# A long-convolution and feed-forward kernel on one core: later start of TensorE in the list, a tile of its own for one sum, and a longer time taken for transposing transfers

## The chip, the core and the metric

The kernel runs on one NeuronCore of a Trainium2 chip. The metric is the time of one execution in device microseconds (us). A core has five engines that run their own instruction queues side by side and wait for one another by semaphores: TensorE (PE; weight loads are shown apart as PEld), VectorE (DVE), ScalarE (ACT), GpSimd (POOL) and SyncE (SP), which here issues most transfers; POOL issues those that add to their destination.

## The reference

```python
x = A_q                                    # 2048 x 1024
xn = _layernorm(x, axis=-1)
return x + _A_ref(xn, A_k, A_v, A_shift_k, A_ssm_k, A_ssm_D) + _B_ref(xn, B_w1, B_w2)
# _A_ref: k_shift = causal depthwise convolution of k with 4 taps; kv = k_shift * v
#         y = causal convolution of kv with ssm_k over the whole length (by FFT) + kv * ssm_D
#         result xn * y
# _B_ref: silu(xn @ w1) @ w2, w1 of 1024 x 3584, w2 of 3584 x 1024
```

## The kernel before

The work is one long program for PE. The two products of the feed-forward part are made in float16 with a high and a low half of each factor: every matmul of 128 x 512 stands three times (lines L1030, L1031, L1032 for the first product, L1183, L1184, L1185 for the second). The first product is made by seven products of sums of blocks, the second is mostly plain. The long convolution goes by group of 128 channels (eight groups): a forward transform on PE (L1670, L1671, L1672), a product of spectra on DVE, a transform back on PE (L1863, L1864, L1865), and a gate. Its work stands between that of the feed-forward part and keeps DVE busy while PE multiplies.

At the start, 16 tiles of 128 rows of x (`xt`) and the pieces of w1 are loaded. DVE takes the statistics of a tile (L565, L568), normalises it (L602), PE transposes it in two times four 128 x 128 steps (L621), ACT and DVE split the result into the high and low float16 halves `x` (L353 is DVE's). The scale of a piece of w1 comes from its sum of squares: ACT makes most of these sums, DVE makes that of the second piece (`squares_dve`, L796, L799, L800) and writes it into one column of the tile `ss`; PE adds them over the partitions (L464, L467), and DVE takes a power of two from it (L508, L510).

The order of all instructions is made when the program is built, by the class `Order`. Each piece of work is a generator, a stream with a bias, and yields operations with an engine, an estimated busy time (`busy`), an estimated time until the result is there (`late`), and the tiles that it reads and writes. In each step the stream with the smallest possible start time less its bias gives its operation, which is emitted at once; the estimates of free engines, written and read cells of 256 bytes, and of one common transfer pipe (`pipe`) are moved on. So the estimates set the order on every engine, and nothing else: on the chip each instruction waits by semaphores for what it needs.

Three places of this matter here.
- Until the first product begins, the list fills gaps that it sees on PE with constant matmuls of 128 x 512 (L1937), `int((t - free - 0.1) / 0.22)` of them before an operation. PE begins with 18 float32 matmuls (`warm_up`, L1934; each is two passes), estimated at 0.3 us.
- Later, before the first matmul of a product, a gap in the estimate is filled in part with matmuls of zeros (L333).
- `X` (L343) is a transfer on SP's queue that transposes: in each group it turns the scaled signal `cm` into the tile `hl`, which PE's forward transform reads. `L` (L338) is a plain transfer on the same queue, which runs in order: wo (halves of the weights), wraw (raw weights), hsfA, hsfS (stores of the first product's result), xg (rows of x for the gate). `G` (L347) is a transfer on POOL's queue that adds a tile to the output, after the gate multiplication `yt` (L353), and after the last step of a part of the second product, `hf`.

A part of the first product ends with ACT copying its banks of PSUM (`hf<-ff`, L361), DVE subtracting or adding another bank to it (`hf<-ff,hf`, L350), ACT's Silu, and a split into halves (`ht`, ACT L361 and DVE L353). The forward transform's banks `ps` are read by ACT (`spec<-ps`) and DVE (`tmp<-tmp,ps`, `spec<-spec,ps`).

Of the kernel before, what the change touches and what calls it, by code (L numbers as in the profile page):

```python
# [11 lines left out]
F32 = mybir.dt.float32  # L12
BF16 = mybir.dt.bfloat16
# [7 lines left out]
P = 128  # L21
# [69 lines left out]
class Op:  # L91


    def __init__(self, eng, busy, late, emit, reads, writes, margin, nbytes=0):
        self.eng, self.busy, self.late, self.emit, self.margin = eng, busy, late, emit, margin
        self.reads, self.writes, self.nbytes = reads, writes, nbytes
        self.table = self.fill = None


class Stream:  # L100
# [5 lines left out]
class Order:  # L106
# [60 lines left out]
    def run(self):  # L167
        while self.streams:
            for s in list(self.streams):
                if not isinstance(s.head, Op) and s.head():  # L170
                    self.advance(s)
            best = None
            for s in self.streams:
                if isinstance(s.head, Op):
                    t = max(self.free[s.head.eng], s.at)
                    if best is None or t - s.bias < best[0]:
                        best = t - s.bias, t, s
            assert best is not None, "the streams wait for one another"
            _, t, s = best
            op, (r, w) = s.head, s.touched  # L180
            if self.spare is not None and op.eng == "PE":
                op.fills = max(0, int((t - self.free["PE"] - 0.1) / 0.22))
                for _ in range(op.fills):
                    self.spare()
            elif op.fill is not None and t > 45.0:
                for _ in range(int(((t - self.free[op.eng]) * 0.7 - 0.3) / 0.22)):
                    op.fill()
            op.emit()
            if op.table not in (None, self.table):
                op.busy += 1.28  # L190
                self.table = op.table
            done = t + op.busy
            end = done + op.late
            if op.nbytes:
                self.pipe = max(self.pipe, t + (2.0 if t < 3.0 else 3.0)) + op.nbytes / (265e3 if t < 3.3 else 330e3)
                done = end = max(end, self.pipe + 0.2)
            self.free[op.eng] = t + op.busy
            for c in r:
                self.read[c] = max(self.read.get(c, 0.0), done)
            for c in w:  # L200
                self.wrote[c] = end, op.eng
            self.now = max(self.now, end)
            self.advance(s)
# [94 lines left out]
def h3_ffn_kernel(ctx, tc, x, kp, vs, fs, shift, dskip, w1, w2, cfwd, cinv, out):  # L298
    nc = tc.nc
    ctx.enter_context(tc.manual_schedule())  # L300
    order = Order()
# [26 lines left out]
    def T(f, o, ins, us, m=0.1, start=None, **kw):  # L328

        p = Op("PE", us, 0.3, f, ins, [o], m)  # L330
        if start is not None:
            z = o[:, 0:1] if len(o.shape) == 3 else o[:, 0:P]
            p.fill = lambda: nc.tensor.matmul(z, zeros, ones, start=start, stop=start, **kw)  # L333
        return p

    def L(o, i, m=0.3):
        n = size(o) * o.shape[0] * mybir.dt.size(o.dtype)
        return Op("SP", 0.4, 0.1, lambda: nc.sync.dma_start(o, i), [i], [o], m, n)  # L338

    def X(o, i, m=0.3):  # L340

        n = size(o) * o.shape[0] * mybir.dt.size(o.dtype)
        return Op("SP", 0.6, 4.0, lambda: nc.sync.dma_start(o, i, transpose=True), [i], [o], m, n)  # L343

    def G(o, i, m=0.3):
        n = size(i) * i.shape[0] * mybir.dt.size(i.dtype)
# [107 lines left out]
    def total(ring, ss, n, margin, joined=False):  # L454

        yield ring.ready
        pt, tok = ring.tile([P, W])
        yield pw.ready
        e, etok = pw.tile([P, 4])
        high = ss.bitcast(BF16)[:, 1::2]  # L460

        def mm():
            if joined:
                nc.tensor.matmul(pt[:, 0:1], onesb, tinyb, start=True, stop=False)  # L464
                for q in range(n):
                    w = manyb if n == 4 and q in (1,) else onesb
                    nc.tensor.matmul(pt[:, 0:1], w, high[:, q:q + 1], start=False, stop=q == n - 1)  # L467
            else:
                nc.tensor.matmul(pt[:, 0:n], onesb, high, start=True, stop=True)
        yield T(mm, pt[:, 0:n], [ss], 0.12 + 0.04 * n * joined, m=margin)  # L470
        return pt, tok, e, etok

    def norm(ring, ss, ns, then, flags, margin=1.5):
# [296 lines left out]
    def load_pair(n):  # L770
# [10 lines left out]
        for a in range(len(pieces)):  # L781
# [7 lines left out]
            yield L(raws[n][2][a], w1r[:, ks, cols])  # L789
            flag["raw", n, a].set()  # L790

    def squares_dve(r, o):
        st = lnp.tile([P, 1, 6], F32, name="wst", bufs=1)
        mean = lnp.tile([P, 2], F32, name="wmean", bufs=1)
        flat = r.rearrange("p k w -> p (k w)")
        yield V(lambda: nc.vector.bn_stats(st[:, 0, :], flat), st, [r], us=0.65)  # L796

        def chain():
            nc.vector.bn_aggr(mean, st)  # L799
            nc.vector.scalar_tensor_tensor(o, mean[:, 0:1], mean[:, 0:1], mean[:, 1:2], op0=MUL, op1=ADD)  # L800
        yield V(chain, o, [st], us=0.45)

    def scales_w1():
        for n, (_, i) in enumerate(pairs):
            yield (0.25, 0.2, 0.1, 0.05)[min(n, 3)]
            m = 4 if n == 0 else 2
            if n >= NP:
                for a in range(m):
                    yield flag["raw", n, a]
                flag["scaled", n].set()  # L810
                continue
            yield sq_r.ready
# [1117 lines left out]
    def warm_up():  # L1930

        pt, tok = ff.tile([P, 4, P])
        for _ in range(18):
            yield T(lambda: nc.tensor.matmul(pt[:, 0, :], ones, ones, start=True, stop=True), pt[:, 0, :], [], 0.3)  # L1934

        def constants():
            nc.tensor.matmul(pt.rearrange("p a b -> p (a b)"), onesb, oneb.to_broadcast([P, W]), start=True, stop=True)  # L1937
        order.spare = constants
        yield flag["first"]
        order.spare = None  # L1940
        tok.set()
# [64 lines left out]
```

## Time and profile before

| | us |
|---|---|
| median of 3 runs | 1242.58 |
| lowest, highest | 1242.13, 1243.62 |
| profiled execution | 1246.58 |
| its span, first to last instruction | 1244.8 |
| PE busy in it | 1230.2 |
| DVE busy in it | 1122.5 |
| ACT busy in it | 741.8 |

The mean granted clock of TensorE is 0.999 of full speed over the span. Times in the views are counted from the span's start. A row of a timeline gives the start, the length, engine, line, operation, output and inputs by the program's names, and in brackets the idle time of the engine before it and what ended that. A row of the waits gives who waited for whom, the total, the count and the longest. A row of the windows gives the stretch, its length, the busy times (and counts) of PE, PEld, DVE, ACT and POOL, the granted clock, the busy share of the transfer engines, and GB/s. A busy matmul is shown with its whole latency, so successive ones overlap: what a matmul costs is the distance from start to start.

### The profile page before, as it was taken

Reading aid. Unit: us, or ns where it says so; the run is one execution under the profiler, and the core shown is the slowest. Engines: PE = TensorE matmul, PEld = TensorE weight load, DVE = VectorE, ACT = ScalarE, POOL = GpSimd, SP = SyncE. Lnnn points to the kernel's source line nnn. Section 1 sums busy time; section 2 is a strip of 40 time slices with the busy share of each in tenths; the row PEclk is TensorE's granted clock in tenths of the full one; section 3 lists DMA queues with packets and bytes.
Section 4 is the critical chain, followed back from the end, with each engine's and each line's share of the span. In section 5 each row is a group of like instructions: output and inputs, shape, how many; then the busy total and the mean of one; then the engine's idle time right before and its main releaser. Section 6 shows DMA issues by size and latency. Waiting matters only on the chain.

```text
span 1244.8 us, 17311 instructions
## 1 busy us (share of the span) xinstructions
PE 1230.2 (99%) x6144; PEld 598.5 (48%) x6144; DVE 1122.5 (90%) x1367; ACT 741.8 (60%) x1299; POOL 142.2 (11%) x164
## 2 busy tenths in 40 slices
PE   9999999999999999999999999999999999999998
PEld 7645544444444544445444544544454454445444
DVE  7999997888799869998999799799989979998993
ACT  6878887877767767768663632653263265426231
POOL 1100000000000120002010300300030030113114
PEclk9999999999999999999999999999999999999999
DMA  9289889889999898969997887788596688978777
GB/s 338 69 267 320 300 299 314 280 276 352 304 350 285 254 246 263 286 208 259 352 315 207 185 244 169 166 263 243 127 220 164 133 177 240 251 144 138 162 150 102
DMA packets 254438, 293.21 MB, mean 236 GB/s; under 512 B 48784, under 2 KB 167824, under 8 KB 252176
## 3 DMA queue, kind: packets, MB, share of 16 engines
q1 hardware_dynamic: 227760, 267.46, 68.6%
q0 software_dynamic: 26592, 24.65, 15.3%
q8 instruction: 48, 0.79, 0.3%
q14 instruction: 38, 0.31, 0.1%
HBM read 193.48 MB, written 98.57 MB: 235 GB/s over the span
## 4 chain that ended last, share of the span: by engine, by line
PE 68%; DVE 19%; DMA 6%; issue 4%; ACT 2%; POOL 0%; SPq 0%; DVEq 0%; ACTq 0%; POOLq 0%
PE ff L1031 10%; PE ff L1030 10%; PE ff L1032 10%; PE ff L1183 10%; PE ff L1184 10%; PE ff L1185 9%; DVE spec L350 7%; DVE tmp L350 3%; DMA hf<-in_w 2%; DVE x L353 2%; PE ps L1670 1%; PE ps L1672 1%; PE ps L1671 1%; DVE spec L353 1%; DMA out<-yt 1%
## 5 line engine op out<-in xcount | busy, mean ns | idle before, releaser
L1183 PE MATMUL ff<-x,wo 128*128 128x512 f16 (+2 forms) x872 | 329.0, 378 | 2.1 <-ACT hf L361 2.1
L1184 PE MATMUL ff<-x,wo 128*128 128x512 f16 (+2 forms) x872 | 329.2, 378 | 0.0
L1185 PE MATMUL ff<-x,wo 128*128 128x512 f16 (+2 forms) x872 | 329.0, 378 | 0.0
L1030 PE MATMUL ff<-x,wo 128*128 128x512 f16 (+2 forms) x840 | 306.7, 367 | 1.8 <-ACT hf L361 1.8
L1031 PE MATMUL ff<-x,wo 128*128 128x512 f16 (+2 forms) x840 | 306.8, 367 | 1.1 <-DVE x L353 1.1
L1032 PE MATMUL ff<-x,wo 128*128 128x512 f16 (+2 forms) x840 | 306.8, 367 | 0.0
L350 DVE TENSOR_TENSOR spec<-spec 128x1024 f32<-128x1024 f32 (+2 forms) x272 | 263.0, 999 | 2.3
L1184 PEld LDWEIGHTS <-wo 128*128 128x128 f16 x872 | 85.4, 98 | 102.1 <-issue 3.2
L1185 PEld LDWEIGHTS <-wo 128*128 128x128 f16 x872 | 85.5, 98 | 101.9 <-issue 0.7
L1183 PEld LDWEIGHTS <-wo 128*128 128x128 f16 x872 | 85.5, 98 | 101.2 <-issue 0.8
L1032 PEld LDWEIGHTS <-wo 128*128 128x128 f16 x840 | 82.2, 98 | 92.0 <-issue 1.2
L1030 PEld LDWEIGHTS <-wo 128*128 128x128 f16 x840 | 82.2, 98 | 88.1 <-issue 0.2
L1031 PEld LDWEIGHTS <-wo 128*128 128x128 f16 x840 | 82.2, 98 | 88.1 <-issue 2.1
L347 POOL DMA_DIRECT2D out<-hf x59 | 52.3, 888 | 449.2 <-ACT hf L361 339.4
L347 POOL DMA_DIRECT2D out<-yt x56 | 63.7, 1359 | 336.9 <-DVE yt L353 192.8
L361 ACT ACTIVATE hf<-ff,invc 128x512 f32<-128x512 f32 x60 | 40.9, 682 | 99.6 <-PE ff L1185 79.0
L350 DVE TENSOR_TENSOR tmp<-spec 128x2048 f32<-128x2048 f32 (+1 forms) x48 | 92.5, 1932 | 0.9
L353 DVE SCALAR_TENSOR_TENSOR ht<-hf,wsc,ht 128x1024 f16<-128x1024 f32 (+1 forms) x56 | 67.3, 1202 | 11.7 <-ACT ht L361 11.5
L361 ACT ACTIVATE spec<-spec 128x1024 bf16<-128x1024 f32 x32 | 33.7, 1054 | 68.5 <-DVE spec L350 68.4
L353 DVE SCALAR_TENSOR_TENSOR wo<-raw,wsc,wo 128x512 f16<-128x512 f32 (+1 forms) x56 | 56.3, 1011 | 12.3 <-ACT wo L361 12.0
L361 ACT ACTIVATE spec<-ps 128x512 f32<-128x512 f32 x96 | 55.0, 589 | 16.3 <-PE ps L1672 15.0
L361 ACT ACTIVATE ht<-hf,wsc 128x1024 f16<-128x1024 f32 (+1 forms) x56 | 60.7, 1085 | 4.7 <-DVE hf L350 3.0
(187 smaller groups left out, 1756.1 us busy)
## 6 DMA issues: line engine op xcount, KB each, us to landing
wo<-hs SPq DMA_DIRECT2D x160, 256.0 KB, 4.0
hs<-ht SPq DMA_DIRECT2D x80, 256.0 KB, 4.4
wraw<-in_w SPq DMA_DIRECT2D x31, 512.0 KB, 5.3
out<-hf POOLq DMA_DIRECT2D x59, 256.0 KB, 4.4
raw<-in_w SPq DMA_DIRECT2D x28, 512.0 KB, 5.9
kin<-in_kp SPq DMA_DIRECT2D x16, 704.0 KB, 5.9
kf<-in_fs SPq DMA_DIRECT2D x8, 1024.0 KB, 5.8
hl<-in_vs SPq DMA_DIRECT2D x32, 256.0 KB, 6.2
```

The costliest lines, as they stand in the source:

```text
L347: return Op("POOL", 1.1, 4.8, lambda: nc.gpsimd.dma_start(o, i, accum_op=ADD), [i], [o], m, n)
L350: return V(lambda: nc.vector.tensor_tensor(o, a, b, op=op), o, [a, b], **k)
L353: return V(lambda: nc.vector.scalar_tensor_tensor(o, a, s, b, op0=op0, op1=op1), o, [a, b] + ([] if isinstance(s, float) else [s]), **k)
L361: nc.scalar.activation(o, i, func, scale=scale, **kw)
L1030: nc.tensor.matmul(o, w[:, 0, k], xf[:, :, k, 0], start=first and k == 0, stop=False, **kw)
L1031: nc.tensor.matmul(o, w[:, 0, k], xf[:, :, k, 1], start=False, stop=False, **kw)
L1032: nc.tensor.matmul(o, w[:, 1, k], xf[:, :, k, 0], start=False, stop=last and k == KH - 1, **kw)
L1183: nc.tensor.matmul(o, hx[:, n, 0, :], wc[:, n, 0, q], start=first and n == 0, stop=False, **kw)
L1184: nc.tensor.matmul(o, hx[:, n, 0, :], wc[:, n, 1, q], start=False, stop=False, **kw)
L1185: nc.tensor.matmul(o, hx[:, n, 1, :], wc[:, n, 0, q], start=False, stop=last and n == 3, **kw)
L1670: nc.tensor.matmul(o, cf[:, 0], hi[i], start=i == 0, stop=False, **kw)
L1671: nc.tensor.matmul(o, cf[:, 0], lo[i], start=False, stop=False, **kw)
```

## The change

Three things are changed. The list takes PE to be free only from 1.0 us on, and a matmul of the warm-up to take 0.36 us and not 0.3. DVE's sum of squares gets a tile of its own, `wsum`, in place of a column of `ss`, so that the list's cell of 256 bytes no longer holds ACT's sums and DVE's at once; PE reads it there. And an operation has a field `extra`, which is added to the end that the transfer pipe gives: 1.0 us for each transposing transfer, 0 for all others.

```diff
@@ class Op
         self.table = self.fill = None
+        self.extra = 0.0
@@ Order.run
             if op.nbytes:
                 self.pipe = max(self.pipe, t + (2.0 if t < 3.0 else 3.0)) + op.nbytes / (265e3 if t < 3.3 else 330e3)
-                done = end = max(end, self.pipe + 0.2)
+                done = end = max(end, self.pipe + 0.2 + op.extra)
@@ h3_ffn_kernel
+    def later(p, extra):
+        p.extra = extra
+        return p
+
     def X(o, i, m=0.3):
-        return Op("SP", 0.6, 4.0, lambda: nc.sync.dma_start(o, i, transpose=True), [i], [o], m, n)
+        return later(Op("SP", 0.6, 4.0, lambda: nc.sync.dma_start(o, i, transpose=True), [i], [o], m, n), 1.0)
@@ total
-                    w = manyb if n == 4 and q in (1,) else onesb
-                    nc.tensor.matmul(pt[:, 0:1], w, high[:, q:q + 1], start=False, stop=q == n - 1)
+                    w, v = (manyb, wsum.bitcast(BF16)[:, 1:2]) if n == 4 and q == 1 else (onesb, high[:, q:q + 1])
+                    nc.tensor.matmul(pt[:, 0:1], w, v, start=False, stop=q == n - 1)
@@ scales_w1
+    wsum = lnp.tile([P, 1], F32, name="wsum")
...
-                    yield from squares_dve(r, ss[:, a:a + 1])
+                    yield from squares_dve(r, wsum)
@@ warm_up
-            yield T(lambda: nc.tensor.matmul(pt[:, 0, :], ones, ones, start=True, stop=True), pt[:, 0, :], [], 0.3)
+            yield T(lambda: nc.tensor.matmul(pt[:, 0, :], ones, ones, start=True, stop=True), pt[:, 0, :], [], 0.36)
@@ the streams
     add(begin(), 0.05)
+    order.free["PE"] = 1.0
     add(warm_up(), 0.0)
```

Counted over the program, 24 constant matmuls (L1937) stand where 31 stood, and three zero fills (L333) where two stood; all other counts are the same. Lines of the changed kernel stand 5 to 8 further down.

The first place is PE's queue at the start, around the transposes of the first row tile (`xt`, two times four steps into `ft`). Before:

```order
L1937 MATMUL ff_217<-oneb 128x512
L621 MATMUL ft_295<-ident,xt_216 128x128 x4
L621 MATMUL ft_322<-ident,xt_216 128x128 x4
L1937 LDWEIGHTS oneb
...
L464 LDWEIGHTS oneb
L464 MATMUL ft_334<-tinyb,oneb 128x1
L467 LDWEIGHTS oneb
L467 MATMUL ft_334<-ss_220,oneb 128x1
L467 LDWEIGHTS many
L467 MATMUL ft_334<-ss_220,many 128x1
```

Now:

```order
L1944 MATMUL ff_218<-oneb 128x512
L626 MATMUL ft_295<-ident,xt_217 128x128 x4
L626 MATMUL ft_318<-ident,xt_217 128x128 x4
L1944 LDWEIGHTS oneb
...
L469 LDWEIGHTS oneb
L469 MATMUL ft_308<-tinyb,oneb 128x1
L472 LDWEIGHTS oneb
L472 MATMUL ft_308<-ss_221,oneb 128x1
L472 LDWEIGHTS many
L472 MATMUL ft_308<-wsum,many 128x1
```

The pieces are the same; what moved is the number of constant matmuls around them, all of which read as the first row does: 13 ahead of the transposes, 6 between them and the sums, 12 behind before, and 4, 2 and 18 now.

The second place is DVE's queue in the middle of the program, from the second gate multiplication of a group on (`yt`; `hf` subtracts a bank of the first product, `ht` is a low half of its result, `spec` and `tmp` are parts of the spectra). Before:

```order
L353 SCALAR_TENSOR_TENSOR yt_3191<-ps_4151,csc_2138,xg_3366 128x512
L350 TENSOR_TENSOR tmp<-tmp,ps_4130 128x2x256
L353 SCALAR_TENSOR_TENSOR zl_4187<-spec,csc_2138,zh_4186 128x1024
L350 TENSOR_TENSOR tmp<-tmp,ps_4137 128x2x256
L350 TENSOR_TENSOR spec<-spec 128x2x512 x2
L353 SCALAR_TENSOR_TENSOR yt_3191<-ps_4185,csc_2138,xg_4162 128x512
L350 TENSOR_TENSOR spec<-spec,ps_4197 128x2x256
L350 TENSOR_TENSOR spec<-spec,ps_4227 128x2x256
L353 SCALAR_TENSOR_TENSOR ht_201<-hf_200,wsc,ht_201 128x8x128
L353 SCALAR_TENSOR_TENSOR yt_3191<-ps_4216,csc_2138,xg_4250 128x512
L350 TENSOR_TENSOR hf_198<-ff_4030,hf_199 128x512
```

Now:

```order
L358 SCALAR_TENSOR_TENSOR yt_3157<-ps_4158,csc_2132,xg_3280 128x512
L358 SCALAR_TENSOR_TENSOR zl_4190<-spec,csc_2132,zh_4189 128x1024
L355 TENSOR_TENSOR tmp<-tmp,ps_4138 128x2x256
L355 TENSOR_TENSOR tmp<-tmp,ps_4145 128x2x256
L355 TENSOR_TENSOR spec<-spec 128x2x512 x2
L358 SCALAR_TENSOR_TENSOR ht_201<-hf_200,wsc,ht_201 128x8x128
L355 TENSOR_TENSOR spec<-spec,ps_4205 128x2x256
L355 TENSOR_TENSOR spec<-spec,ps_4220 128x2x256
L355 TENSOR_TENSOR hf_198<-ff_4015,hf_199 128x512
L358 SCALAR_TENSOR_TENSOR yt_3157<-ps_4188,csc_2132,xg_4169 128x512
```

The third yt now stands behind ht, two sums and hf, all of which stood behind it before; the fourth comes five rows further down.

The third place is SP's queue around a group's last transposing transfer, at the passage from the first product to the second (`wraw` are raw weights, `wo` halves of weights, `hsfA` and `hsfS` stores of results). Before:

```order
L338 DMA hsfA_69<-ht_201 128x4x256
L338 DMA xg_5242<-in_x 128x2x128 x2
L343 DMA_TRANSPOSE hl_2134<-cm 128x8x128
L338 DMA wraw_3192<-in_w 128x2x512
L338 DMA hsfA_72<-ht_202 128x4x256
L338 DMA wo_194<-hs_73 128x1024 x2
L338 DMA hsfS_67<-ht_201 128x4x256
```

Now:

```order
L339 DMA hsfA_69<-ht_201 128x4x256
L339 DMA wraw_3158<-in_w 128x2x512
L339 DMA hsfA_72<-ht_202 128x4x256
L339 DMA wo_194<-hs_73 128x1024 x2
L339 DMA xg_5246<-in_x 128x2x128 x2
L348 DMA_TRANSPOSE hl_2129<-cm 128x8x128
L339 DMA hsfS_67<-ht_201 128x4x256
```

The transfer and the load of xg ahead of it moved behind a load of raw weights, a store and two loads of weights.

More of the change, by code (lines that the diff above doesn't have):

```diff
@@ L465, in mm @@
                 for q in range(n):
-                    w = manyb if n == 4 and q in (1,) else onesb
-                    nc.tensor.matmul(pt[:, 0:1], w, high[:, q:q + 1], start=False, stop=q == n - 1)
+                    w, v = (manyb, wsum.bitcast(BF16)[:, 1:2]) if n == 4 and q == 1 else (onesb, high[:, q:q + 1])
+                    nc.tensor.matmul(pt[:, 0:1], w, v, start=False, stop=q == n - 1)
             else:
                 nc.tensor.matmul(pt[:, 0:n], onesb, high, start=True, stop=True)
-        yield T(mm, pt[:, 0:n], [ss], 0.12 + 0.04 * n * joined, m=margin)
+        yield T(mm, pt[:, 0:n], [ss, wsum] if n == 4 else [ss], 0.12 + 0.04 * n * joined, m=margin)
         return pt, tok, e, etok
```

## The prediction

> **What bounds the kernel now.** I read the page first: its busy times and its chain.
>
> ```profile
> PE 1230.2 (99%) x6144; PEld 598.5 (48%) x6144; DVE 1122.5 (90%) x1367; ACT 741.8 (60%) x1299; POOL 142.2 (11%) x164
> ...
> PE 68%; DVE 19%; DMA 6%; issue 4%; ACT 2%; POOL 0%; SPq 0%; DVEq 0%; ACTq 0%; POOLq 0%
> ```
>
> TensorE (PE) is busy for 99% of the span. Its matmuls do not get faster by this change, so only two things can move the time: matmuls that fall away, and waits of PE that go or come. Hence the second view, the waits of PE over the whole span.
>
> ```profile
> PE ps L1670 <- ACT tmp L361: 2.7, 2, 1.7
> PE ff L1183 <- ACT hf L361: 2.1, 1, 2.1
> PE ff L1030 <- ACT hf L361: 1.8, 1, 1.8
> PE ff L1031 <- DVE x L353: 1.1, 1, 1.1
> PE ff L1934 <- DVE oneb L404: 1.1, 1, 1.1
> PE ps L1670 <- DVE tmp L350: 0.7, 1, 0.7
> PE ps L1670 <- DVE yt L353: 0.3, 1, 0.3
> ```
>
> Seven rows, 9.8 us in all. That is the whole stake of the re-ordering; anything better needs fewer matmuls. The third view is PE's timeline at the start, where the change takes matmuls away.
>
> ```profile
> 1.06 6.61 PE L1934 MATMUL ff<-one 128*128 128x128 f32 x36 [1.06 <-DVE oneb L404]
> 7.51 3.00 PE L1937 MATMUL ff<-oneb 128*128 128x512 bf16 x13
> 10.35 1.04 PE L621 MATMUL ft<-ident,xt 128*128 128x128 f32 x8
> 11.22 1.47 PE L1937 MATMUL ff<-oneb 128*128 128x512 bf16 x6
> 12.53 0.17 PE L464 MATMUL ft<-tinyb,oneb 128*128 128x1 bf16 x1
> ...
> 12.66 2.78 PE L1937 MATMUL ff<-oneb 128*128 128x512 bf16 x12
> 15.28 1.03 PE L621 MATMUL ft<-ident,xt 128*128 128x128 f32 x8
> 16.15 0.22 PE L1030 MATMUL ff<-x,wo 128*128 128x128 f16 x1
> ...
> 19.32 0.22 PE L1031 MATMUL ff<-x,wo 128*128 128x128 f16 x1 [1.10 <-DVE x L353]
> ```
>
> The columns are start, length, line, operation, count. From 7.51 to 16.15 PE never idles, but 31 of its matmuls (13, 6 and 12 of L1937) compute nothing: they are put in while the list believes that PE has nothing to do.
>
> **Term 1: the start.** The order of the changed kernel has 4, 2 and 18 constants in the three places. One costs (10.35 - 7.51) / 13 = 0.218 us from start to start. DVE's timeline tells whether the data are there earlier:
>
> ```profile
> 7.31 0.80 DVE L602 TENSOR_SCALAR xt<-xt,ln 128x1024 f32<-128x1024 f32 x1
> ...
> 9.00 1.40 DVE L565 BATCH_NORM_STATS2 st<-xt 128x6 f32<-128x512 f32 x2 [0.55 <-DMA xt<-in_x]
> ...
> 13.46 0.69 DVE L353 SCALAR_TENSOR_TENSOR x<-ft,x 128x512 f16<-128x512 f32 x1 [0.23 <-ACT xt L361]
> 14.07 0.81 DVE L602 TENSOR_SCALAR xt<-xt,ln 128x1024 f32<-128x1024 f32 x1
> ```
>
> The first tile is normalised at 7.31 + 0.80 = 8.11, and the eight transposes wait behind constants until 10.35. With four constants they start at 7.51 + 4 x 0.218 = 8.38, take 11.22 - 10.35 = 0.87, and end at 9.25; two constants and the norm (0.44 + 0.13) bring PE to 9.82, where the norm before was at 12.53. Eighteen constants then fill to 9.82 + 3.92 = 13.74. Is the second tile ready by then? DVE now does half of the statistics (0.7) from 9.00, the first low half of x (0.69), the other statistics, the small norm steps, the second low half (0.69) and the normalisation (0.81): some 4.2 us of work in a row, 13.2 at best, against 14.88 before. So the constants, not DVE, release the transposes, at 13.74 instead of 15.28: **-1.53 us** (7 x 0.218). The first product L1030 moves from 16.15 by as much, and the wait of 1.10 at 19.32 hangs on DVE work behind the same transposes and moves along. A little more is possible, since DVE is ahead by 1.7 and PE by 1.5: I bound this term by -2.0. On the other side it could be 0, if an input lands too late (a rival below).
>
> The own tile for DVE's sum of squares (`wsum`) only frees the list from a dependence that it saw inside one 256-byte cell; the instructions are the same length, so it costs 0 by itself. The three zero matmul fills (L333) in place of two:
>
> ```profile
> L333 PE MATMUL ff<-one,zero x4: 273/273/275, 316.7 to 317.0; 128*128 128x128 f32 x4
> ```
>
> Four passes lie between 316.7 and 317.0, about 0.11 us each, two to a fill. One fill more is **+0.22 us**; all three now stand near 568 and not at 316, so 0.45 is gained early and 0.67 spent late.
>
> **Term 2: the waits at 441 and 455.** Only between 283 and 990 us does the larger completion time re-order anything. DVE, ACT, PE and the chain of waits between 430 and 457:
>
> ```profile
> 442.25 8.19 DMA out<-yt
> ```
>
> ```profile
> 431.35 0.75 DVE L353 SCALAR_TENSOR_TENSOR yt<-ps,csc,xg 128x512 f32<-128x512 f32 x1
> ...
> 440.54 0.75 DVE L353 SCALAR_TENSOR_TENSOR yt<-ps,csc,xg 128x512 f32<-128x512 f32 x1 [2.65 <-DMA out<-yt]
> ...
> 450.62 0.75 DVE L353 SCALAR_TENSOR_TENSOR yt<-ps,csc,xg 128x512 f32<-128x512 f32 x1 [3.39 <-DMA out<-yt]
> 451.28 0.68 DVE L350 TENSOR_TENSOR hf<-ff,hf 128x512 f32<-128x512 f32 x1
> ```
>
> ```profile
> 452.00 1.15 ACT L361 ACTIVATE hf<-hf,wsc 128x1024 f32<-128x1024 f32 x1 [3.20 <-DVE hf L350]
> ...
> 456.31 0.57 ACT L361 ACTIVATE hf<-ff 128x512 f32<-128x512 f32 x1
> ```
>
> ```profile
> 454.72 0.38 PE L1032 MATMUL ff<-x,wo 128*128 128x512 f16 x1
> 456.94 0.38 PE L1030 MATMUL ff<-x,wo 128*128 128x512 f16 x1 [1.84 <-ACT hf L361]
> ```
>
> The third and fourth gate multiplications (yt) wait for the store of the one before, which is out of the way only 440.54 - 431.35 = 9.2 us after it began (8.19 of a transfer in the chain's row). DVE runs in order: behind the fourth stands the subtraction hf, behind it ACT, behind that the bank which PE wants. So a store costs PE 456.94 - 454.72 - 0.22 = 2.00 us, and the third yt, on whose bank PE waits at 441, 0.45. In the changed order hf stands **ahead** of both, and the work that followed the third yt (the subtractions of two products, one ht) stands ahead of it too. Counting PE's rows there at 0.216 us a matmul, with the 1.53 and 0.45 that PE is ahead, the product that hf reads is complete near 442, so hf runs near 443 and ACT's step some 9 us before 452.00. The third yt comes after about 6.7 us more of DVE work, and the store has landed. The fourth may still wait (the store behind it lands near 452), but behind it stand only spectrum sums, no bank of PE. **-2.45 us**.
>
> What is late next? After 456 DVE hardly rests:
>
> ```profile
> 460.00:520.00 60.00, 60.00 (x281) 27.20 (x280) 59.76 (x69) 41.19 (x73) 0.00 (x0) 1.00 0.83 256
> 520.00:580.00 60.00, 59.32 (x295) 28.61 (x294) 58.41 (x76) 41.36 (x65) 2.20 (x2) 1.00 0.80 236
> ```
>
> The third busy column is DVE's: 59.76 of 60, then 58.41. There PE's lead lasts only if DVE has it too. Of its idle time before 456 DVE loses 1.5 with the start and, by its rows, the 2.65 at 440; it reaches the same work about 4 us earlier, as PE does. So I leave the later waits (0.7 and 1.0 at 578 and 688, 1.7 at 900, 2.1 at 1085) as they are: PE's order after 690 is nearly the same, and these hang on DVE and ACT alone.
>
> **Sum.** -1.53 - 2.45 + 0.22 = -3.76 us. The profiled execution took 1246.58 (span 1244.8, 1.8 around it), which becomes 1242.8. It lies 4.0 above the median of the runs, 1242.58; part of that is this:
>
> ```profile
> 1088.00:1092.00 4.00, 4.00 (x12) 1.49 (x11) 3.96 (x5) 0.00 (x0) 0.88 (x1) 0.57 0.55 70
> ```
>
> ```profile
> 1088.14 0.63 PE L1184 MATMUL ff<-x,wo 128*128 128x512 f16 x1
> ...
> 1091.13 0.52 PE L1185 MATMUL ff<-x,wo 128*128 128x512 f16 x1
> ```
>
> After the 2.12 us of waiting at 1085 the granted clock falls to 0.57 for some 3 us: seven starts take 2.99, 0.427 each and not 0.216, about 1.7 us lost in all. After the 1.84 at 455 there was no such loss. I carry the difference over to the median unchanged: 1242.58 - 3.76 = **1238.8 us**.
>
> [...]
>
> **Rivals.**
>
> *DVE keeps what PE wins* (0.18). If DVE meets 456 only 1.5 us earlier, the two waits at 578 and 688 grow by the 2.45 and only the start remains: 1242.58 - 1.53 + 0.22 = 1241.3. For it speak the windows above; against it that DVE's idle time at 440 is before the subtraction and shrinks in the new order.
>
> *The start does not do what it says* (0.12). An input still in flight could hold the first product, PE then idling where constants were. The row at 9.00 shows DVE waiting 0.55 for such a transfer. Then 1242.58 - 2.45 + 0.22 = 1240.35, and with term 2 lost as well (half of this case) 1242.8.
>
> *More goes* (0.10). The list now gives each transposing transfer a later end, so work that needs one stands later; the waits at 578 and 688 (0.7 and 1.0) could go too: 1238.8 - 1.7 = 1237.1.
>
> *The sync queue blocks the weights* (0.20), the case on the other side. SP's queue is in order, and near 562 to 575 the changed order puts a weight load, a store of ht parts and two loads of wo ahead of the transposing transfer and its xg.
>
> ```profile
> SPq L338 <- DVE ht L353: 5.6, 3, 2.2
> ```
>
> ```profile
> wo<-hs SPq DMA_DIRECT2D x160, 256.0 KB, 4.0
> ```
>
> A store waits up to 2.2 us for its ht; what stands behind it then needs 4.0 us to land (a wo) or more (the transfer). Here, at the passage from the first product to the second, where all loads are ordered anew, PE would wait 2.2 + 4.0 = 6.2 us once the lead of the weights is used up, and with the slow clock after it 1.7 more: 1238.8 + 6.2 = 1245.0 to 1246.7. It decides from the point at which a wo lands after its matmul's turn. Against it: no wait of PE on a transfer stands among the seven rows; and the moved transfer, issued near 572.5 - 4 in the changed order, is used some 10 us later.
>
> **How the numbers follow.** The forecast has 0.40, the rivals 0.18, 0.12, 0.10 and 0.20. A measurement of this kernel can tell about 0.2%, 2.5 us, from no change. Faster by more than that: the forecast, "more goes", and a quarter of the start rival, 0.53. Within it: "DVE keeps", the rest of the start rival, 0.27. Slower: 0.20. The range goes down to "more goes" with the start at its bound of -2.0 (1236.6) and up to the lower price of the blocked queue (1245.1), leaving out less than 2 in 10.
>
> **What would show it.** Term 1: eight transposes near 8.4 and again near 13.7, and the first L1030 near 14.6. Term 2: no row of PE waiting for ACT hf with L1030, none for DVE yt, and hf ahead of a waiting yt. "DVE keeps": the rows of PE on tmp grow to 4 us. The queue: a row of PE or of its weight loads on DMA wo. I am wrong if a wait of PE over 2 us stands where none was, or if the first L1030 still starts near 16.

## The result and the profile after

The changed kernel takes 1239.08 us (median of 9 runs, 1237.92 to 1240.01), beside 1242.58 (1239.97 to 1245.04, 9 runs) of the kernel before on the same chip. The ratio is 0.9968 with the 95% interval [0.9958, 0.9978]: 4.0 us faster (2.7 to 5.2; the two medians differ by 3.5), where 3.76 were forecast. The sum came out; several of its terms did not. The profiled execution took 1238.71, its span is 1236.9.

The page of the changed kernel, busy times and chain:

```profile
PE 1226.6 (99%) x6139; PEld 596.5 (48%) x6139; DVE 1123.5 (91%) x1367; ACT 742.1 (60%) x1299; POOL 142.0 (11%) x164
...
PE 90%; DVE 6%; DMA 2%; issue 1%; ACT 1%; SPq 0%; DVEq 0%; ACTq 0%
```

The chain that ended last runs through PE for 90% of the span and not for 68% (90% and 65% in a second execution of each): fewer detours over DVE. All waits of PE after the change (who waits for whom; total, count, longest):

```profile
PE ft L626 <- DVE xt L607: 1.4, 1, 1.4
PE ff L1038 <- DVE x L358: 1.4, 1, 1.4
PE ff L334 <- ACT hf L366: 1.2, 1, 1.2
PE ff L1941 <- DVE oneb L409: 1.1, 1, 1.1
PE ps L1677 <- ACT tmp L366: 0.6, 1, 0.6
```

They add up to 5.7 us, before to 9.8. The rows of hf with the first product, of yt, of DVE's tmp and of the 2.1 us are gone; the first and the third row are new. PE's start in the same trace:

```profile
1.06 5.96 PE L1941 MATMUL ff<-one 128*128 128x128 f32 x36 [1.06 <-DVE oneb L409]
6.85 1.03 PE L1944 MATMUL ff<-oneb 128*128 128x512 bf16 x4
9.32 1.09 PE L626 MATMUL ft<-ident,xt 128*128 128x128 f32 x8 [1.43 <-DVE xt L607]
...
10.81 4.10 PE L1944 MATMUL ff<-oneb 128*128 128x512 bf16 x18
14.75 1.03 PE L626 MATMUL ft<-ident,xt 128*128 128x128 f32 x8
15.62 0.22 PE L1037 MATMUL ff<-x,wo 128*128 128x128 f16 x1
```

4 and 18 constants stand where 13 and 12 stood (2 for 6 between them), but PE idles 1.43 us ahead of the first transposes, and the first product begins at 15.62, not near 14.6. DVE shows why:

```profile
7.86 0.69 DVE L803 BATCH_NORM_STATS2 wst<-x 128x6 f32<-128x512 f32 x1 [2.57 <-DMA x<-in_w]
8.47 0.80 DVE L607 TENSOR_SCALAR xt<-xt,ln 128x1024 f32<-128x1024 f32 x1
```

The normalisation of the first tile (L607) stands in DVE's queue behind the statistics of a piece of w1 (L803), and that piece landed late here. The middle, DVE:

```profile
444.39 0.69 DVE L355 TENSOR_TENSOR spec<-spec,ps 128x512 f32<-128x512 f32 x1 [3.19 <-ACT spec L366]
445.00 0.68 DVE L355 TENSOR_TENSOR hf<-ff,hf 128x512 f32<-128x512 f32 x1
445.60 0.74 DVE L358 SCALAR_TENSOR_TENSOR yt<-ps,csc,xg 128x512 f32<-128x512 f32 x1
...
454.75 0.74 DVE L358 SCALAR_TENSOR_TENSOR yt<-ps,csc,xg 128x512 f32<-128x512 f32 x1
```

hf runs at 445.00 where it ran at 451.28, and neither gate multiplication waits for a store. A new wait stands at 570, PE first, then ACT:

```profile
570.63 0.38 PE L1039 MATMUL ff<-x,wo 128*128 128x512 f16 x1
572.26 0.94 PE L334 MATMUL ff<-one,zero 128*128 128x128 f32 x6 [1.25 <-ACT hf L366]
573.03 0.38 PE L1037 MATMUL ff<-x,wo 128*128 128x512 f16 x1
```

```profile
570.09 1.14 ACT L366 ACTIVATE zh<-spec,csc 128x1024 f16<-128x1024 f32 x1
571.13 0.59 ACT L366 ACTIVATE spec<-ps 128x512 f32<-128x512 f32 x1
571.61 0.60 ACT L366 ACTIVATE hf<-ff 128x512 f32<-128x512 f32 x1
```

The copy of the bank (hf) stands behind two pieces of the convolution on ACT. PE waits 1.25 us for it, and the three zero fills (six passes) come after the wait, where they fill nothing: 573.03 - 570.63 - 0.22 = 2.18 us in one place. This was not foreseen.

### The profile page after: what moved, and what is told of

Its sections match the earlier page's. It is cut to its first block, busy times and chain, and to the rows that moved or that the text cites. A ratio compares the mean times of both kernels' runs of the same rounds, so it can differ in the third digit from the quotient of the medians.

```text
span 1236.9 us, 17306 instructions
## 1 busy us (share of the span) xinstructions
PE 1226.6 (99%) x6139; PEld 596.5 (48%) x6139; DVE 1123.5 (91%) x1367; ACT 742.1 (60%) x1299; POOL 142.0 (11%) x164
## 4 chain that ended last, share of the span: by engine, by line
PE 90%; DVE 6%; DMA 2%; issue 1%; ACT 1%; SPq 0%; DVEq 0%; ACTq 0%
PE ff L1037 13%; PE ff L1038 13%; PE ff L1039 13%; PE ff L1190 13%; PE ff L1192 13%; PE ff L1191 13%; PE ps L1677 2%; PE ps L1679 2%; PE ps L1678 2%; DVE spec L355 2%; DVE tmp L355 1%; PE ps L1870 1%; PE ps L1872 1%; PE ps L1871 1%; PE ft L626 1%; DVE x L358 1%
## 5 line engine op out<-in xcount | busy, mean ns | idle before, releaser
L358 DVE SCALAR_TENSOR_TENSOR acc<-kin,taps,acc 128x1024 f32<-128x1024 f32 x48 | 61.4, 1278 | 4.4 <-ACT acc L366 4.4
```

The lines of the kernel that those rows point to most:

```text
L358: return V(lambda: nc.vector.scalar_tensor_tensor(o, a, s, b, op0=op0, op1=op1), o, [a, b] + ([] if isinstance(s, float) else [s]), **k)
```

## The experiments

Every kernel was timed beside the kernel before, on the same chip; the differences in us are the ratio less one, times that kernel's median. "Lost" is the distance between the starts of two successive matmuls of PE, less the 0.216 us (0.056 for the narrow ones at 17) of a matmul that does not wait (in before, 128x512 from 470 to 474 us and 128x128 from 16.15 to 16.77). For the profiled executions it is:

| PE loses near | before | before, again | changed | changed, again |
|---|---|---|---|---|
| 7.5 (first transposes) | 0 | 0 | 1.59 | 0 |
| 17 (low half of x) | 1.26 | 1.26 | 1.54 | 1.54 |
| 441 | 0.45 | 0 | 0 | 0.48 |
| 455 | 2.00 | 1.09 | 0 | 0 |
| 570 (and the fills after it) | 0 | 0 | 1.41 | 1.41 |
| 577 | 0.84 | 0.43 | 0 | 0 |
| 687 | 1.18 | 0.73 | 0 | 0 |
| 900 | 1.84 | 1.29 | 0 | 0 |
| 1083 | 2.28 | 2.12 | 0 | 0.67 |
| 1120 | 0 | 0.39 | 0.81 | 0.80 |

**Two executions of one order.** Edit: none (the kernel before, once more).

> The kernel before, unchanged, for a second profile. Theory A (the waits that the first profile shows late in the program belong to the order): the waits of TensorE at 900 (1.8 us) and 1085 (2.1 us, with a granted clock of 0.57 behind it) stand there again, and the span is near 1244. Theory B (they come and go from run to run): at least one of the two is gone or under 1 us, the clock does not fall, and the span is 2 to 5 us shorter. Both expect the waits at 441 and 455 again.

Measured: 1241.29 us, span 1239.5. Its waits:

```profile
PE ff L1183 <- ACT hf L361: 2.0, 1, 2.0
PE ps L1670 <- ACT tmp L361: 1.9, 3, 1.1
...
PE ff L1030 <- ACT hf L361: 0.9, 1, 0.9
```

The places are the same but for 441, the sizes are not: 455 lost 1.09 instead of 2.00, and 441 nothing. At 900 and 1083 the waits stand again, as theory A has it, but the clock does not fall behind them and the span is 5.3 us shorter, as theory B has it. Most waits belong to the order of the queues; their size belongs to the execution. The prediction rested on a long execution (1246.58 with a median of 1242.58, and above all 9 runs beside the changed kernel), and its waits are the larger ones.

**The two halves of the change.** Each alone, and both:

```diff
# start_only: the changed kernel without the longer transfer
-        return later(Op("SP", 0.6, 4.0, ...), 1.0)
+        return later(Op("SP", 0.6, 4.0, ...), 0.0)
# extra_only: the changed kernel with the start of before
-    order.free["PE"] = 1.0
-... pt[:, 0, :], [], 0.36)      (warm-up)
+... pt[:, 0, :], [], 0.3)
-                    yield from squares_dve(r, wsum)
+                    yield from squares_dve(r, ss[:, a:a + 1])
# after_again: the changed kernel, unchanged
```

The first has the start of the changed kernel and the later order of before, the second the reverse, instruction for instruction.

> Only the start of the change: TensorE free from 1.0, 0.36 us for a warm-up matmul, the own tile for the sum; no longer time for transposing transfers, so all queues after the start stand as before. Theory of the prediction: seven constant matmuls at 0.218 are saved, -1.5 us, first L1030 product near 14.6. Rival (from the profile after): the first row tile is normalised behind DVE's statistics of a weight piece, which waits for that piece's transfer; TensorE idles 1 to 1.6 us ahead of the transposes where constants stood, and only 0 to 0.7 us is saved.

> Only the longer time of transposing transfers in the list: the start as before (31 constants), all queues after about 283 us as in the changed kernel. Theory of the prediction: the waits at 441 and 455 go, one zero fill more, -2.2 us. Rival: the re-ordering gives back what it wins at a new wait near 570 (1.4 us in the profile after), so -1 us or less; second rival: the order after 690 is better too (waits at 688, 900 and 1085 gone), -4 us or more.

> The changed kernel, unchanged, for a second profile and beside the two parts on one chip. Theory of the prediction: the parts add up, about -3.5 us. If the wait of 1.4 us ahead of the first transposes comes from the run and not from the order, it is under 0.5 us here; if it belongs to the order it stands again. The wait near 570 (ACT hf) is expected to stand again, 1 to 1.5 us.

Measured, beside 1243.40 (16 runs): start_only 1242.89, ratio 0.9993 [0.9984, 1.0002], so -0.9 us (-2.0 to +0.2); extra_only 1239.17, 0.9971 [0.9959, 0.9982], -3.6; both 1238.21, 0.996 [0.9948, 0.9973], -5.0. The parts add up within their intervals, and most is in the later order. The interval of start_only holds both of its theories. For extra_only the second rival came nearest: the waits at 577, 687 and 900 are gone and 0.50 is left at 1081. In the profile of start_only the old waits stand, and a new one, the first row (2.34 lost at 1131):

```profile
PE ps L1677 <- ACT spec L366: 2.2, 1, 2.2
PE ff L1190 <- ACT hf L366: 1.8, 1, 1.8
PE ps L1677 <- ACT tmp L366: 1.7, 4, 0.8
```

Beside the same work in the second execution of before, PE is 0.59 us ahead at 25 us, 0.78 at 470 and 0.06 at 600: a lead from the start goes into the next wait for DVE or ACT. The start itself, in the changed kernel's second execution:

```profile
7.42 1.03 PE L1944 MATMUL ff<-oneb 128*128 128x512 bf16 x4
8.29 1.03 PE L626 MATMUL ft<-ident,xt 128*128 128x128 f32 x8
...
14.53 0.22 PE L1037 MATMUL ff<-x,wo 128*128 128x128 f16 x1
```

Transposes at 8.29 and the product at 14.53, as forecast (8.4 and 14.6). From the first constant to the first product it is 7.11 us, in both executions of before 8.64: 1.53 less. Where the first tile is late it is 15.62 - 6.85 = 8.77, and nothing is gained. Eight profiles have this start; in three (the changed kernel, extra_2_0, dve_tax6_862) PE lost 0.99 to 1.59 us ahead of the first transposes, in two some 0.2, in three nothing.

**The third gate multiplication moved.** In the kernel before, the third yt of that group is not given to the list before the hf behind it has been emitted:

```diff
+            self.counts[op.eng] += 1          # in Order.run, after op.emit()
...
+            if (g, t) == (0, TO[2]):
+                yield lambda: order.counts["DVE"] >= 529
             yield v_stt(flat[0], flat[1], sc[:, 5:6], flat[2], MUL, MUL)
```

The list after 441 us is made anew by this; up to 690 it differs from both kernels, behind 690 it is the changed kernel's but for a few swaps of neighbours and three pieces near 1077. So this run changes more than one step.

> The kernel before with one thing added: the third gate multiplication (yt, near 440 us on VectorE) is given only after the subtraction hf has been given; the list orders what follows from there by its old numbers (no longer time for transposing transfers, old start). Theory of the prediction (hf behind a waiting yt makes the waits at 441 and 455): both go, -2 us or more, whatever the order behind them is. As the list falls back into the changed kernel's order after 690, the waits at 900 and 1085 should go with them if that order is their cause: -4 us in all. Rival (VectorE is the bound from 456 on): the wait only moves to 578 or 688 and the time stays within 1 us.

Measured: 1241.05 beside 1242.76 (31 runs), 0.9985 [0.9974, 0.9995], -1.9 us (-3.2 to -0.6).

```profile
PE ff L1185 <- ACT hf L363: 2.0, 1, 2.0
PE ff L1032 <- ACT hf L363: 1.5, 1, 1.5
```

Nothing is lost at 441 and 455 any more, and the step stands for 455: that wait comes from a store that holds a gate multiplication with hf behind it. In every profile in which hf does not stand behind a waiting yt (this one, the changed kernel, extra_only), nothing is lost there. For 441 it is not shown: in the second execution of before yt waits 2.33 us for its store and PE loses nothing, and in the changed kernel's second one PE loses 0.48 there on DVE's spec. The 1.9 us are not these two waits alone either: those at 577, 687 and 900 are gone too, while 1082 stays (2.19 lost) and new ones stand at 575 (1.71, again hf on ACT coming late at the passage between the products), 911 and 1010 (0.42 and 0.69).

**ACT's place near 803.** There DVE waits much longer before than after. Before, and after:

```profile
810.50 0.69 DVE L350 TENSOR_TENSOR spec<-spec,ps 128x512 f32<-128x512 f32 x1 [6.39 <-ACT spec L361]
```

```profile
805.75 0.69 DVE L355 TENSOR_TENSOR spec<-spec,ps 128x512 f32<-128x512 f32 x1 [3.54 <-ACT spec L366]
```

Before, ACT waits here for a load of xg, with three pieces (two copies and a multiplication) and then spec behind it:

```profile
806.25 0.49 ACT L361 ACTIVATE xg<-xg,nmr,rstd 128x128 f32<-128x128 f32 x1 [2.33 <-DMA xg<-in_x]
```

In the changed order the xg stand behind spec. The experiment moves the first of them in the kernel before; from 831 us on the list makes another order after that:

```diff
+                            if (g, t, b, i) == (4, TO[2], 0, 0):
+                                yield lambda: order.counts["ACT"] >= 829
                             yield a_act(xg[:, b, i], xg[:, b, i], AF.Identity, ...)
```

> The kernel before with one thing added: the first normalisation of a tile xg near 803 us on ScalarE, which waits there for its transfer with two copies, a multiplication and two bank reads behind it, is given only after those. Everything up to 798 us stands as before. Theory (this one wait in ScalarE's queue makes VectorE late by 2 to 3 us and so the waits at 900 and 1085): VectorE's wait of 6.4 us near 807 shrinks to about 3.5, the wait at 900 goes, that at 1085 goes or halves and the clock does not fall there: -2 to -4 us. Rival (those waits come from VectorE's place before 690): they stand as before, within 0.7 us of the kernel before.

Measured: 1242.86 beside 1242.76, 0.9997 [0.9986, 1.0009]: no gain.

```profile
803.15 1.06 ACT L363 ACTIVATE hl<-kf 128x1024 bf16<-128x1024 f32 x1 [1.92 <-DMA kf<-in_dskip]
```

```profile
806.89 0.69 DVE L352 TENSOR_TENSOR spec<-spec,ps 128x512 f32<-128x512 f32 x1 [5.49 <-ACT spec L363]
```

The next piece in ACT's queue waits for a transfer of its own, and DVE still waits 5.49. This one step is not what gains the 3 us there. Which step of the changed order does is open; it is not the start, since start_only has 6.63 in this row, and the kernels whose order there is the changed one's or nearly so (extra_only, extra_0_5, hold_yt, the changed one, norm_nofill of the next experiment) have 3.2 to 3.5.

**The two new waits taken away.** The changed kernel, with the first tile normalised ahead of the weight piece's statistics, and without zero fills:

```diff
-            elif op.fill is not None and t > 45.0:
-                ...
+        yield flag["xn", 0]                   # in squares_dve
         yield V(lambda: nc.vector.bn_stats(st[:, 0, :], flat), st, [r], us=0.65)
```

> The changed kernel with the first row tile normalised on VectorE ahead of the statistics of the weight piece, and without the three zero fills, which compute nothing. Theory (the start's saving is lost where the normalisation waits behind a weight piece's transfer): TensorE is idle for under 0.3 us ahead of the first transposes in the profile, and the zero fills cost 0.67 us behind the wait at 570: together 0.5 to 2 us below the changed kernel, about -5 us against the kernel before. Rival (the transposes are held elsewhere, or the fills lie inside the wait): no difference from the changed kernel, -3.5 to -4.

Measured: 1238.54 beside 1242.76, 0.9965 [0.9951, 0.9978], -4.3; the changed kernel's 0.9968 and 0.996 lie within. The normalisation waits for nothing but its own statistics, of which POOL makes the last step (ln), and PE no longer waits ahead of the transposes:

```profile
6.20 0.81 DVE L604 TENSOR_SCALAR xt<-xt,ln 128x1024 f32<-128x1024 f32 x1 [1.03 <-POOL ln L577]
```

```profile
7.84 0.82 PE L1942 MATMUL ff<-oneb 128*128 128x512 bf16 x3
8.50 1.03 PE L623 MATMUL ft<-ident,xt 128*128 128x128 f32 x8
```

At 570 the wait stays at 1.41 without the fills. What the fills (573.03 - 572.26 = 0.77 us) and the sometimes late tile save is less than the intervals can tell.

**Other sizes of the longer time.** 2.0 and 0.5 us in place of 1.0, as `extra` of each transposing transfer:

> The changed kernel with 2.0 us in place of 1.0 for each transposing transfer. Theory A (the numbers are nearer to the transfers, which land after 3.1 to 9.9 us with a median of 5.5, so loads and their users stand better): as good as 1.0 or better, -3.5 to -6 us. Theory B (any other number makes another order, good or bad by where single waits fall): the time may lie anywhere from -4 to +4 us, and its waits stand at other places than those of 1.0.

Measured: 1239.25 beside 1242.76, 0.9971 [0.9961, 0.9982], -3.6, as with 1.0. This order does not compute the reference's result, so it is no kernel to use, and only its waits are read: PE loses 1.33 us ahead of the first transposes and 1.11 at 566, and again nothing over 0.4 us between 580 and the end. That longer times are truer ones, as theory A has it, is not borne out: the 31 transposing transfers landed 4.5 us after their issue in before and 4.0 in the changed kernel (medians; the 5.5 of the text counts plain loads into hl too), and the list allows 0.6 + 4.0 us even without the extra time. The half size:

> The changed kernel with 0.5 us in place of 1.0 for each transposing transfer; at 441 and 455 us the third gate multiplication again stands behind the subtraction, other pieces between 280 and 530 us stand differently on ACT and VectorE. Theory 'any order that puts the subtraction first gains': within 1 us of the changed kernel's 1238.2 to 1239.1, with no wait of TensorE near 441 and 455 and VectorE again some 7 us ahead of before at 850. Rival 'this one order was luck': a wait of over 1 us returns somewhere between 441 and 1085 and the time is 1240.5 to 1242.5.

Measured: 1240.55 (10 runs) beside 1242.22 (22 runs), 0.9991 [0.9978, 1.0003].

```profile
PE ff L1190 <- ACT hf L366: 1.8, 1, 1.8
...
PE ps L1677 <- DVE spec L355: 1.1, 1, 1.1
```

The wait at 1081 is back (1.96 lost) and there is one at 444 (1.26); waits and time (1240.55) are those of the rival. The interval, -2.7 to +0.4 us, begins where the changed kernel's (-5.2 to -2.7) ends. Not every order that puts hf first has the gain: the order that 1.0 makes is a lucky one.

**The wait at 1083.** Behind 690 the queues of hold_yt and extra_0_5 are those of the changed kernel but for a few swaps of neighbours (pieces of cm, some matmuls) and three pieces near 1077: a sum (tmp) and an x on DVE, an x on ACT. Both lose here (2.19 and 1.96), as before and start_only do; the changed kernel and extra_only lose 0.67 at most. In the second execution of before, and of the changed kernel, ACT runs:

```profile
1080.61 0.72 ACT L361 ACTIVATE x<-x,tau 128x512 f16<-128x512 f32 x1 [1.02 <-DVE x L350]
1081.23 0.67 ACT L361 ACTIVATE hf<-ff,invc 128x512 f32<-128x512 f32 x1
```

```profile
1077.74 0.67 ACT L366 ACTIVATE hf<-ff,invc 128x512 f32<-128x512 f32 x1
1078.31 0.71 ACT L366 ACTIVATE x<-x,tau 128x512 f16<-128x512 f32 x1
```

The copy hf, for which PE waits, stands behind a second x that DVE delivers late in the first order and ahead of it in the second. DVE is as far ahead of PE at 890 in extra_0_5 as in the changed kernel (2.0 us beside before, again, in both), so it is this swap, and not a lead, that takes most of the wait away.

**Does DVE have room?** The prediction left the waits at 688, 900 and 1085 as they were, and in the changed kernel's two profiles they are gone or small. To see whether DVE's lead decides them, useless statistics go into DVE's queue of the changed kernel, everything else in its order:

```diff
+    taxo = cst.tile([P, 6], F32, name="taxo")
+    def tax():
+        for _ in range(6):                    # 12 in dve_tax12
+            nc.vector.bn_stats(taxo, one.to_broadcast([P, W]))
...
+            if op.eng == "DVE" and self.counts["DVE"] == 850:   # 950 in dve_tax6_862
+                self.tax()
```

> The changed kernel with six statistics of a constant (128 x 512 each, their result is read by nobody) put into VectorE's queue near 862 us, about 6 x 0.61 = 3.7 us of added VectorE work; every other instruction on every queue stands as in the changed kernel. Theory 'VectorE's lead decides': the waits of TensorE near 900 and 1085 are gone in the changed kernel because VectorE reaches the work at 850 some 7 us earlier than before and is never late for a bank after it; with 3.7 us taken from that lead they come back in part, 0.5 to 1.5 us near 900 or 1080, and the time rises by 0.5 to 3 us over the changed kernel, to 1239 to 1241.5. Rival 'the order itself': the waits went because other work stands first in the queues; then nothing comes back, and with VectorE idle for 9% of the span the time stays within 0.5 us of the changed kernel's 1238.2 to 1239.1.

> The same with twelve of them, about 7.3 us of added VectorE work near 862 us, as much as the lead that VectorE has over the kernel before at 850 to 895 us. Theory 'VectorE's lead decides': the waits near 900 (1.0 to 1.7 us) and near 1080 (about 2 us, with the fallen clock behind it up to 1.7 more) come back whole, and the time rises by 3 to 6 us over the changed kernel, to 1241.5 to 1245, at least the time before. Rival 'the order itself': within 1 us of the changed kernel's.

The lead of 7 us in these texts is too large: at 850 the changed kernel's DVE is 3.1 us ahead of the same work of before in the second executions, 5.4 in the first. The count of 850 put the statistics one group earlier than the texts say, at 764 us, where six took 4.33 us. PE's waits with six, then with twelve:

```profile
PE ps L1688 <- ACT tmp L370: 3.1, 2, 2.5
...
PE ps L485 <- ACT spec L370: 1.0, 1, 1.0
```

```profile
PE ps L485 <- ACT spec L370: 4.7, 1, 4.7
PE ps L1688 <- ACT tmp L370: 1.7, 2, 1.0
```

Measured: six 1242.87 and twelve 1246.64 beside 1242.22; ratios 1.0002 [0.9992, 1.0011] and 1.0035 [1.0023, 1.0047], so +0.2 and +4.3 us over before, where the changed kernel stands at -4.0 to -5.0. 4.33 us of DVE work cost 4.2 to 5.2 us, twice as much 8.3 to 9.3: at 764 DVE has no room at all. PE loses 3.84 us at 773 and 787 with six (1.20 and 2.64), 6.00 with twelve. The same six at the place that was meant:

> The changed kernel with the six statistics (6 x 0.72 = 4.3 us of VectorE, as they took in dve_tax6) at the place meant there: near 862 us, one group later than they stood in dve_tax6 and dve_tax12, where they were at 764. At 764 the added 4.3 us came back as 3.8 us of waits of TensorE. Theory 'VectorE's lead decides': at 862 VectorE has the 7 us that it gains over the kernel before, of which some 4 are unused, so less comes back than at 764: a wait of 0.5 to 2 us near 900 and 0.5 to 2 near 1085, 1239.5 to 1242. Rival 'VectorE has no room anywhere': the whole 4.3 us come back as at 764, 1242.5 to 1243.5. Rival 'the order itself': no wait comes back, within 0.5 us of the changed kernel's 1238.2 to 1239.1.

```profile
863.33 4.33 DVE L429 BATCH_NORM_STATS2 taxo<-one 128x6 f32<-128x512 f32 x6
```

```profile
PE ps L1688 <- ACT tmp L370: 4.1, 3, 2.5
```

Measured: 1243.35 (10 runs) beside 1241.02 (13 runs), 1.0014 [1.0005, 1.0024], +1.7 over before, 5.7 to 6.7 over the changed kernel. The wait at 900 is back (2.63 lost, 0.60 at 885); 1085 loses 0.39. Between 880 and 920 PE falls back by 4.9 us beside the changed kernel's second execution, more than was added, since the clock (the column after POOL's) falls after the wait:

```profile
901.00:905.00 4.00, 3.64 (x15) 1.80 (x15) 3.29 (x5) 3.19 (x6) 0.06 (x1) 0.71 0.82 129
```

This profile is the slowest of its ten runs, and not all of its lateness is the added work: up to 863 its queues are the changed kernel's, yet PE had lost 1.12 at 687 and 0.83 at 800 by then. So the wait at 687 is not gone for good from this order.

Why the wait at 900 comes and goes can be read from two rows, here of the second execution of before: a step of DVE on the spectra, and PE's first matmul of the next forward transform, which waits for ACT's copies (tmp) behind that step:

```profile
892.89 2.36 DVE L353 SCALAR_TENSOR_TENSOR spec<-spec 128x1024 f32<-128x1024 f32 x2
```

```profile
898.59 0.38 PE L1670 MATMUL ps<-hl,cfw 128*128 128x512 f16 x1 [1.13 <-ACT tmp L361]
```

| profile | DVE's step begins | PE's matmul begins | distance | PE lost |
|---|---|---|---|---|
| before | 896.45 | 902.15 | 5.70 | 1.84 |
| before, again | 892.89 | 898.59 | 5.70 | 1.29 |
| start_only | 892.47 | 898.16 | 5.69 | 0.98 |
| hold_xg | 891.85 | 897.54 | 5.69 | 0.59 |
| hold_yt | 892.13 | 897.82 | 5.69 | 0.02 |
| changed | 890.86 | 897.21 | 6.35 | 0 |
| changed, again | 889.63 | 896.39 | 6.76 | 0 |
| dve_tax6 | 893.56 | 900.29 | 6.73 | 0 |
| dve_tax6_862 | 895.67 | 901.36 | 5.69 | 2.63 |

In every profile of the table that loses here PE begins 5.7 us after DVE's step, before and after the change; where PE gets there later than that, it loses nothing. So what decides is how far DVE is ahead of PE, and not how early either is: in dve_tax6 DVE is later than in before, again, but PE has been held up as well. The room that DVE has here is 0.7 to 1.1 us in the changed kernel (6.35 and 6.76 less 5.69), not the 4 that I expected.

## Why the prediction came out, step by step

- **The stake** (waits of PE of 9.8 us are all that a new order can win): held as a bound. 4.1 us of waits went, net, between the first profiles, 2.4 between the second ones.
- **Term 1, the start, -1.53.** The distance is right to the hundredth wherever the first tile is ready, and the second transposes begin when the 18 constants end, as "the constants, not DVE, release the transposes" says. The step that failed is the one before it, "With four constants they start at" 8.38: the row of DVE's normalisation at 7.31 was read as fixed, but it stands behind the statistics of a weight piece, whose landing moves between executions (they began at 6.25 to 7.86). Before, the 13 constants covered this; four do not. And part of the lead ends in later waits. Alone it is worth -0.9 (-2.0 to +0.2).
- **Term 2, the waits at 441 and 455, -2.45.** The mechanism was right for 455: hf stands ahead of yt in the rows, and nothing is lost there in any order that has it so. The size was that of one long execution; in the second one before it would have been 1.09. No run gives it a price by itself, since hold_yt (-1.9, -3.2 to -0.6) changes other waits too.
- **The zero fills, +0.22.** Right as a count and as a place, and 0.77 us for the 0.67 said; but they stand behind a wait of 1.41 which the sum did not have. That no new wait comes in failed at 570, by ACT's copy hf behind two pieces of the convolution. Wait and fills take 2.18 us in this place.
- **DVE's place.** That DVE reaches the work behind 456 "about 4 us earlier, as PE does" failed: at 520 it is 0.7 us ahead between the second executions (PE 1.9), 2.2 between the first (PE 3.4).
- **The later waits "as they are".** This step failed most: 577, 687, 900 and 1083 lost 6.14 and 4.57 us in the two executions before, 0 and 0.67 after (extra_only has 0.5 left, at 1081); 1120 takes 0.81 and 0.80 where it took 0 and 0.39. I had compared PE's order after 690, found it nearly the same, and said that the waits "hang on DVE and ACT alone": they do, and the orders of ACT, SP and DVE differ in places from 707 us on, near 1077 too. DVE's wait near 805 shrinks from 6.4 to 3.5 us by that, and DVE goes from 0.4 us behind the same work at 800 to 3.1 ahead at 850 (second execution of each; 1.8 and 5.4 ahead in the first), while PE is only 0.9 ahead. The distances above show for 900 that this is what takes the wait away. At 1083 it is the swap on ACT.
- **The sum.** Between the second executions of both, PE's gain on the same work is 1.93 us at 470, -0.25 at 575, 0.90 at 700, 2.19 at 920 and 2.82 at the end: won, given back at 570, and won again by what I had called unchanged. The forecast size is right by luck: less was won up to 470 than forecast, a wait not foreseen took that away, and waits that were to stay gave it back.
- **The rivals.** "More goes" was the nearest: the waits at 578 and 688 went as it says, 900 and 1085 with them. "DVE keeps" described rightly that DVE is full from 456 on, yet the new order gave DVE 3 us. "The start does not do what it says" happened in three of eight profiles. The blocked sync queue did not: no row of PE or of a weight load waits for a transfer of wo.

## What to carry to other kernels

Read the orders of all engines, not that of the bound engine, before calling a late wait unchanged: a wait of PE with DVE or ACT behind it goes or comes with their queues, a few us ahead of it (1083) or some 100 us ahead (900). An engine that is busy 91% on average (DVE in the changed kernel) can be without any room in one stage (4.33 us added at 764 cost 4.2 to 5.2); the test is a few microseconds of useless work put there. And take the size of a wait from more than one execution, since the place is that of the order but the size was 1.09 in one and 2.00 in another.

## What the runs showed of the hardware that was not expected

- The warm-up of 36 passes takes 5.6 to 7.2 us from profile to profile (5.64 in extra_only, 7.21 in dve_tax6; 5.96 in the row above, 6.61 before), and PE's first useful matmul moves with it: with the start of before the first product begins at 15.18 behind 5.64 us (extra_only) and at 16.32 behind 6.77 (hold_yt), 1.14 later, where the change at the start was to win 1.53. In windows of 1 us PE has 6 or 7 passes each from 2 to 6 us in before and 11 from 6 to 7; in the changed kernel 7 each from 2 to 4, 8 from 4 to 5, then 12 and 11. What changes the pace is not shown.
- After PE has lost 2 us or more in a wait the clock falls in some profiles and not in others: after the 2.28 of before near 1083 it fell to 0.57 over 1088 to 1092, after the 2.19 of hold_yt to 0.50 over 1085 to 1088, and after the 2.63 at 898 in dve_tax6_862 to 0.71 over 901 to 905; after the 2.12 of the second execution of before, the 2.34 at 1131 in start_only, and the 2.64 at 787 in dve_tax6 it stayed at 1.00. The row of dve_tax6 behind that wait:

```profile
790.00:794.00 4.00, 4.00 (x29) 2.64 (x27) 3.77 (x6) 3.73 (x7) 0.87 (x1) 1.00 0.47 85
```

The length of a wait alone does not decide it: 2.64 us stand without a fall and 2.19 with one. What does is open.
